# Leaky ReLU as one ScalarE activation, and the sign of float64 weights brought by the same function

## The chip, the core and the metric

The kernel runs on one core of a Trainium2 chip. The core has five engines that work side by side, each taking its own instructions strictly in order: TensorE (PE: matrix products, with PEld for its weight loads), VectorE (DVE), ScalarE (ACT), GpSimd (POOL) and SyncE (SP, which here only issues DMAs). They wait for each other by semaphores. The metric is the device time of one execution in microseconds, as the median of several runs.

## The reference

Three stages follow each other: a gated linear attention (batch 2, 8 heads, 768 steps, head size 40), a gated feed-forward part (320 to 1536 to 320) and a leaky-ReLU feed-forward part (320 to 2048 to 320), over 1536 tokens.

```python
# attention, per step t
m_new = np.maximum(f_gate[:, :, t] + m, i_gate[:, :, t])
C = f_stab[:, :, None, None] * C + i_stab[:, :, None, None] * np.einsum('bhd,bhe->bhde', vt, kt)
y[:, :, t] = o * h_tilde / denom
# first feed-forward part
g = xn @ w_gate
silu = g * (1.0 / (1.0 + np.exp(-g)))
x = silu * (xn @ w_val) @ w_out
# second feed-forward part
h = x @ w_in
g = np.maximum(0.01 * h, h)
return (g @ w_out).astype(np.float32)
```

The weights come as float64 and are turned into float32 on the core.

## The kernel before

Attention is done in 12 tiles of 128 tokens of one batch (`T` = 0 to 11), the feed-forward parts in 4 groups `g` of 384 tokens. All products are float32; in the feed-forward parts each factor is split in a high and a low part, so that one product is several matmuls.

**Attention tile.** PE makes scores `s` from `qkt`; ACT makes decay weights `w` from `Ab` (which POOL has masked), DVE multiplies `s` into `w`; PE makes `o` from `w`, `nat` and the state `Cbd`; DVE and ACT normalise it (`sm`, `y`, `junk`), POOL finishes the norm (`sm`), DVE makes `xn`, PE transposes it into `tp`, ACT and DVE copy it into `xt`. Between products of the first tiles PE gets filler products (`busy`) that nothing reads.

**First feed-forward part** (`ffn1`). For each 128 hidden columns `f` PE makes `g` and `v` (8 matmuls each), ACT a tanh `th`, DVE two products, ACT the high part `sh`, DVE the low part `sl`, and PE adds them with `wB` into `xa`. The first four `f` of each group run between the attention tiles, the other eight after them.

**Second feed-forward part** (`ffn2`). For each `f` PE makes `h` (8 matmuls), `u` is made from it, ACT makes the high part `gh`, DVE the low part `gl`, and PE adds 9 matmuls `oa`.

**Weight conversion** (`to_f32`). A float64 word arrives as two 32-bit halves in `raw` (`raw_A` 128x512, `raw_R` 128x256, `raw_B` 128x320; each has two buffers, loaded in turn by SP). DVE shifts the low half into `w32` (called `w_A`, `w_R`, `w_B` in the profile); DVE puts the sign bit of the high half to it; ACT changes the exponent of the high half in place; DVE shifts that and puts it to `w32`. Then ACT rounds it to the high part and DVE makes the low part. 58 such conversions are made: 20 of A, 10 of R, 28 of B. With `gate[0]`, the first DVE step of a conversion is kept behind an earlier DVE instruction; the ACT step is not.

**Order.** The first part is written out by hand (`HEAD`, as a manual schedule). Behind it `BODY` is a written order too, but a scheduler with its own estimate of times merges it, and all that follows, into one order for each engine, bound by data and by buffers; so any change in the instructions moves others.

Of the kernel before, what the change touches and what calls it, by code (L numbers as in the profile page):

```python
# [7 lines left out]
F32 = mybir.dt.float32  # L8
# [3 lines left out]
AF = mybir.ActivationFunctionType  # L12
# [61 lines left out]
class Engine:  # L74
    """An engine whose last instruction can be looked up, and whose next ones can be kept behind an earlier one."""

# [13 lines left out]
def body(ctx: ExitStack, tc, ig, fg, qk, nat, wgv, wgr, wo1, wi2, wi2r, wo2, rg, cst, cst2, out):  # L90
# [27 lines left out]

    # ---- constants
    ident = const.tile([128, 128], F32, name="ident")  # L120
# [12 lines left out]

    # ---- gates
    gt = [wpool.tile([16, 2, NC, L], F32, tag="wA", name=f"gt{i}") for i in range(5)]
# [12 lines left out]
    def busy(n, dst=None, start=True):  # L148
        """Keeps the tensor engine's clock up; nothing reads what it writes."""
        if n and dst is None:  # L150
            dst = psum("busy", "acc")
        for _ in range(n):
            PE.matmul(dst, idle[0], idle[1][:, 0:dst.shape[1]], start=start, stop=start)

    # F and a local to each chunk, and A over them, for chunks c0 to c1
    def scan_f(c0, c1):
# [62 lines left out]

    # ---- attention, one tile of 128 tokens of one batch at a time  # L220
    st_ = [dict() for _ in range(NTILE)]
# [29 lines left out]

    # even heads at rows 0-39 and odd heads at rows 64-103 run in different row tiles, so in different banks
    def att_qk(T, tag="s"):
# [59 lines left out]
    def att_av(T, fill=0, mid=0):  # L313
        c, b = divmod(T, B)
        t = st_[T]
        vn = t["vn"]
        o1 = psum(f"o1_{T}", "o", 2)
        spare = o1[:, H * V1:]
        t["num"] = num = o1[:, 0:H * V1].rearrange("p (h d) -> p h d", h=H)
        # one accumulation over the bank: its first product clears, the others find their columns clear  # L320
        if c > 0:
            for p in range(4):
                PE.matmul(
                    o1[:, p * 2 * V1:(p + 1) * 2 * V1], t["eb"][0:104, p, :], Cbd[b][:, p, :],
                    start=(p == 0), stop=False,
                )
            busy(mid, spare, False)
        for e in range(2):
            for p in range(4):
                PE.matmul(  # L330
                    num[:, 2 * p + e], t["w"][e][:, p, :], vn[:, 2 * p + e, :], start=(c == 0),
                    stop=(c == 0 or (e == 1 and p == 3)),
                )
                if p % 2:
                    busy(fill, spare, c == 0 or (e == 1 and p == 3))
        if c < NC - 1:
            st = o1[:, H * V1:]
            for h in range(H):
                p, e = divmod(h, 2)
                lo, hi = (0, 64) if e == 0 else (64, 104)  # L340
                PE.matmul(st[lo:hi, p * V1:(p + 1) * V1], Kt[b][:, p, lo:hi], vn[:, h, :], start=True, stop=True)
            t["stv"] = st[0:104, 0:4 * V1].rearrange("p (j d) -> p j d", j=4)
# [12 lines left out]

    # normaliser, output gate, 1 / sqrt(mean(y^2) + 1e-6)
    def att_tanh(T):
# [167 lines left out]
    def conversion(key, f):  # L525
        """The next step of one conversion; the last one leaves the weight complete."""
        if (key, f) not in convs:
            if key == "A":
                convs[key, f] = weight_a(f, raws[f][0], raws[f][1])
            else:  # L530
                convs[key, f] = weight_b(f, raws[f][2])
        return convs[key, f]
# [43 lines left out]

    # ---- weights: float64 words rounded toward zero to float32, then split in two parts that add up to it
    def load_raw(src, n, name):
# [4 lines left out]
    def to_f32(raw, n, name):  # L583
        lo, hi = raw[:, :, 0], raw[:, :, 1]
        w = conv.tile([128, 512], U32, tag="w32", name=f"w32_{name}")[:, 0:n]
        first = V.tensor_scalar(out=w, in0=lo, scalar1=29, scalar2=None, op0=ALU.logical_shift_right)
        after(first, gate[0])
        V.scalar_tensor_tensor(out=w, in0=hi, scalar=0x80000000, in1=w, op0=ALU.bitwise_and, op1=ALU.bitwise_or)
        # exponent bias 1023 -> 127, three places to the right of where float32 has it
        A.activation(hi.bitcast(F32), hi.bitcast(F32), AF.Abs, scale=2.0 ** -112)  # L590
        yield
        V.scalar_tensor_tensor(out=w, in0=hi, scalar=3, in1=w, op0=ALU.logical_shift_left, op1=ALU.bitwise_or)
        return w.bitcast(F32)
# [8 lines left out]
    def weight_a(key, raw, raw_rest):  # L602
        """256 columns of the first 256 rows; with every second, the last 64 rows of two such."""
        w = slot("wA", [128, 2, 3, 256], key % NF, f"wA_{key}")
# [20 lines left out]
    def weight_b(key, raw):  # L625
        x = yield from to_f32(raw, DM, f"B{key}")
        if key < NF:
            # high 0:256, low 256:576, high of the last 64 columns
            w = slot("wB", [128, 2 * DM], key, f"wB_{key}")
# [13 lines left out]
    def up(dst, w, m, X):  # L643
        """dst[128 m, N] = w[:, m tile].T @ x, with x and w in two parts each."""
        ms = slice(m * 128, (m + 1) * 128)
        seq = [
            (w[:, 0, 0, ms], X[:, 0]), (w[:, 0, 0, ms], X[:, 3]),
            (w[:, 0, 1, ms], X[:, 1]), (w[:, 0, 1, ms], X[:, 4]),
            (w[:, 1, 0, ms], X[:, 0]), (w[:, 1, 1, ms], X[:, 1]),
            (w[:, 0, 2, ms], X[:, 2]), (w[:, 1, 2, ms], X[:, 2]),  # L650
        ]
        for i, (a, x) in enumerate(seq):
            PE.matmul(dst, a, x, start=(i == 0), stop=(i == len(seq) - 1))

    # ---- first feed-forward part for one group
    def ffn1(g, f0, f1):
        X = xt[g]
        def terms(f, sh, sl, i):
            w = WB[f]
            if i < 2:  # L660
                wh, wl = w[:, i * 128:(i + 1) * 128], w[:, 256 + i * 128:384 + i * 128]
                return [(wh, sh), (wh, sl), (wl, sh)]
            # high and low parts of the last 64 columns side by side
            wr = w[:, 512:640]
# [58 lines left out]
        def finish():  # L723
# [4 lines left out]
            if f1 == NF:  # L728
                # the last 64 columns came in two halves
                tmp = ffn.tile([64, N], F32, tag="th", name=f"tmp{g}")  # L730
# [16 lines left out]
    def ffn2(g, f0, f1):  # L747
# [25 lines left out]
        for f in range(f0, f1):  # L773
# [3 lines left out]
            u = ffn.tile([128, N], F32, tag="th", name=f"u{g}_{f}")  # L777
            A.mul(u, ph[:, 0:N], 0.01)
            V.tensor_tensor(u, ph[:, 0:N], u, op=ALU.max)
            sh = ffn.tile([128, N], F32R, tag="sh", name=f"gh{g}_{f}", bufs=SB)  # L780
# [13 lines left out]

    # ---- the whole
    def load1(f):
# [42 lines left out]
def _layout(np, q, k, v, i_gate, f_gate, o_gate, moe_w_gate, moe_w_val, moe_w_out, moe_rms_g, moe2_w_in, moe2_w_out):  # L839
# [3 lines left out]
    def headsT(a):  # L843
        # [c, b, e (head in pair, padded to 64), d, pair, t]
        t = np.zeros((NC, B, 2, 64, 4, L), f32)
# [14 lines left out]
    def up(w):  # L860
        # [320, n, 256] -> the first 256 rows [n][128][k, m], and the last 64 of two n [n / 2][(n, row)][m]
        n = w.shape[1]
# [47 lines left out]
```

## Time and profile before

| | |
|---|---|
| runs (3), device time | 497.24, 502.96, 504.24 us; median 502.96 |
| profiled execution, first to last instruction | 502.2 us; mean granted TensorE clock 0.968 |
| PE busy | 487.8 us (97%), 3026 instructions |
| DVE busy | 345.7 us (69%), 715 instructions |
| ACT busy | 257.3 us (51%), 610 instructions |
| POOL busy | 82.3 us (16%), 130 instructions |

The profile is of one execution. Nothing but its span is known of its own time, so the sum is made against the span, which lies 0.76 us under the median of the runs. A busy PE can be a slow one: the column PEclk tells what share of the full TensorE clock was granted, 1.00 being the level of 2.4 GHz and 0.50 that of 1.2 GHz.

### The profile page before, as it was taken

How to read it: one execution, taken by the hardware profiler on the slowest of the kernel's cores; microseconds unless marked ns; L12 is line 12 of the kernel's file. 1: busy time of each engine (PE TensorE's matmuls, PEld its weight loads, DVE VectorE, ACT ScalarE, POOL GpSimd, SP SyncE). 2: the span in 40 equal slices, each digit the busy share in tenths (PEclk: the TensorE clock that was granted, in tenths of full speed). 3: DMA queues.
4: the chain of work that ended last, by engine and by line, in shares of the span. 5: the costliest groups of instructions: out<-in, count | busy, mean ns of one | idle time of the engine just before them, and what ended most of it. 6: DMA issues, size and time to landing. Idle time of an engine off the chain costs nothing.

```text
span 502.2 us, 8186 instructions
## 1 busy us (share of the span) xinstructions
PE 487.8 (97%) x3026; PEld 468.8 (93%) x3029; DVE 345.7 (69%) x715; ACT 257.3 (51%) x610; POOL 82.3 (16%) x130
## 2 busy tenths in 40 slices
PE   9998799999979999999999999999999999999996
PEld 5785689889979999999999999999999999999996
DVE  5686778799995798867758486768675834545343
ACT  1243577657663667634626272458575643433332
POOL 2375365675532000000000000000000000000000
PEclk9999896987989999999999999999999999999999
DMA  6855399576310224320302030202301000101011
GB/s 208 288 191 187 111 317 266 190 210 198 109 54 15 82 77 132 115 70 0 116 2 94 1 115 1 94 1 94 96 2 52 1 1 1 40 0 41 1 39 40
DMA packets 31113, 45.90 MB, mean 91 GB/s; under 512 B 2161, under 2 KB 20513, under 8 KB 31073
## 3 DMA queue, kind: packets, MB, share of 16 engines
q1 hardware_dynamic: 31072, 45.38, 28.4%
q8 instruction: 24, 0.39, 0.3%
q14 instruction: 17, 0.13, 0.1%
HBM read 43.31 MB, written 2.06 MB: 90 GB/s over the span
## 4 chain that ended last, share of the span: by engine, by line
PE 85%; DVE 8%; ACT 2%; issue 2%; DMA 1%; POOL 1%; DVEq 0%; POOLq 0%; SPq 0%; ACTq 0%
PE h L82 18%; PE oa L82 17%; PE g L82 13%; PE v L82 12%; PE xa L82 12%; PE o L82 7%; PE s L82 3%; PE busy L82 2%; DMA nat<-nat 1%; DVE w_B L82 1%; POOL sm L82 1%; DVE w_R L82 1%; DVE wB L82 1%; DVE xn L82 1%; PE A L82 1%
## 5 line engine op out<-in xcount | busy, mean ns | idle before, releaser
L82 PE MATMUL h<-xt,wA 128*128 128x384 f32 x512 | 102.0, 337 | 0.0
L82 PE MATMUL g<-xt,wA 128*128 128x384 f32 x384 | 85.7, 353 | 4.0 <-ACT xt L82 3.7
L82 PEld LDWEIGHTS h<-xt,wA 128*128 128x128 f32 x512 | 88.9, 188 | 0.0
L82 PE MATMUL v<-xt,wA 128*128 128x384 f32 x384 | 80.2, 343 | 0.0
L82 PE MATMUL oa<-wB,gh 128*128 128x320 f32 x384 | 77.1, 308 | 0.0
L82 PEld LDWEIGHTS g<-xt,wA 128*128 128x128 f32 x384 | 71.2, 199 | 5.6 <-ACT xt L82 4.2
L82 PEld LDWEIGHTS v<-xt,wA 128*128 128x128 f32 x384 | 70.7, 196 | 0.0
L82 PE MATMUL xa<-sh,wB 128*128 128x384 f32 x240 | 69.6, 343 | 0.8 <-DVE wB L82 0.8
L82 DVE TENSOR_TENSOR u<-h,u 128x384 f32<-128x384 f32 x64 | 35.4, 555 | 41.7 <-ACT u L82 41.5
L82 PEld LDWEIGHTS oa<-wB,gh 128*128 128x128 f32 x384 | 63.2, 188 | 0.0
L82 ACT ACTIVATE u<-h 128x384 f32<-128x384 f32 x64 | 31.5, 492 | 49.8 <-PE h L82 46.4
L82 DVE TENSOR_TENSOR gl<-u,gh 128x384 fp32r<-128x384 f32 x64 | 35.5, 556 | 26.1 <-ACT gh L82 26.0
L82 PE MATMUL oa<-wB,gl 128*128 128x320 f32 x192 | 49.3, 309 | 0.0
L82 PE MATMUL xa<-sl,wB 128*128 128x384 f32 x144 | 48.5, 337 | 0.0
L82 ACT CAST gh<-u 128x384 fp32r<-128x384 f32 x64 | 32.7, 515 | 27.4 <-DVE u L82 27.3
L82 PEld LDWEIGHTS xa<-sh,wB 128*128 128x128 f32 x240 | 44.6, 192 | 1.5 <-DVE wB L82 1.1
L82 ACT ACTIVATE th<-g 128x384 f32<-128x384 f32 x48 | 23.4, 488 | 36.2 <-PE g L82 31.9
L82 DVE SCALAR_TENSOR_TENSOR th<-th,g 128x384 f32<-128x384 f32 x48 | 26.3, 549 | 19.8 <-ACT th L82 19.4
L82 ACT CAST sh<-th 128x384 fp32r<-128x384 f32 x48 | 24.4, 512 | 28.7 <-DVE th L82 25.3
L82 DVE TENSOR_TENSOR sl<-th,sh 128x384 fp32r<-128x384 f32 x48 | 28.5, 599 | 9.6 <-ACT sh L82 9.5
L82 PEld LDWEIGHTS oa<-wB,gl 128*128 128x128 f32 x192 | 33.7, 188 | 0.0
L82 DVE SCALAR_TENSOR_TENSOR w_B<-raw_B,w_B 128x320 uint32<-128x320 uint32 x56 | 30.1, 548 | 4.7 <-ACT raw_B L82 4.5
(90 smaller groups left out, 711.2 us busy)
## 6 DMA issues: line engine op xcount, KB each, us to landing
raw_B<-wo SPq DMA_DIRECT2D x28, 320.0 KB, 3.3
qkt<-qk SPq DMA_DIRECT2D x12, 512.0 KB, 4.9
raw_A<-wgv SPq DMA_DIRECT2D x12, 512.0 KB, 3.9
nat<-nat SPq DMA_DIRECT2D x12, 484.0 KB, 5.1
Ab<-A_d SPq DMA_DIRECT2D x11, 512.0 KB, 6.5
raw_A<-wi SPq DMA_DIRECT2D x8, 512.0 KB, 3.5
eb<-e_d SPq DMA_DIRECT2D x20, 128.0 KB, 5.7
out<-x SPq DMA_DIRECT2D x12, 160.0 KB, 1.9
```

What stands on the lines that cost most here:

```text
L82: self.last = getattr(self.engine, name)(*args, **kwargs)
```

## The change

`u` in `ffn2` was made by ACT (0.01 times `h`) and DVE (the larger of that and `h`). Now one ACT instruction, a leaky activation with slope 0.01 (`Prelu`), reads `h` and writes `u`.

In `to_f32` the DVE step with the sign bit is left out. The ACT step, which took the absolute value times 2^-112, is now a leaky activation with slope -(2^32): a negative word comes out positive with 32 more in its exponent, and the last DVE step, a shift left by three places, moves that bit to the place of the sign. Loads, products and the other instructions are the same in kind and number.

```diff
@@ def to_f32
         first = V.tensor_scalar(out=w, in0=lo, scalar1=29, scalar2=None, op0=ALU.logical_shift_right)
         after(first, gate[0])
-        V.scalar_tensor_tensor(out=w, in0=hi, scalar=0x80000000, in1=w, op0=ALU.bitwise_and, op1=ALU.bitwise_or)
...
-        A.activation(hi.bitcast(F32), hi.bitcast(F32), AF.Abs, scale=2.0 ** -112)
...
+        A.activation(hi.bitcast(F32), hi.bitcast(F32), AF.Prelu, scale=2.0 ** -112, alpha=-(2.0 ** 32))
         yield
         V.scalar_tensor_tensor(out=w, in0=hi, scalar=3, in1=w, op0=ALU.logical_shift_left, op1=ALU.bitwise_or)
@@ def ffn2
             u = ffn.tile([128, N], F32, tag="th", name=f"u{g}_{f}")
-            A.mul(u, ph[:, 0:N], 0.01)
-            V.tensor_tensor(u, ph[:, 0:N], u, op=ALU.max)
+            A.activation(u, ph[:, 0:N], AF.Prelu, alpha=0.01)
```

The scheduler's order moves with it. PE's instructions are the same in kind and number, in another order; ACT has the same number of instructions, DVE 122 fewer. The first places where an engine's order differs lie in the part that is written by hand, for an ACT step that waits for its load alone can stand between the instructions of that part.

**PE where the last attention tile's `o1_11` is made** (`s11`, `tp9`, `o1` belong to attention, the rest to the first feed-forward part). Before:

```order
L82 MATMUL s11_1_1627<-qkt11_1555 128x128
L82 MATMUL tp9_1639<-ident_87,xn9_1636 128x128 x3
L82 MATMUL o1_11_1664<-Cbd1_98,eb11_1559 128x82 x4
L82 MATMUL g2_0_1680<-xt2_1158,wA_0_445 128x384 x8
L82 MATMUL xa1_0_0_1706<-sh1_2_1527,wB_2_949 128x384
L82 MATMUL v2_0_1689<-xt2_1158,wA_0_445 128x384 x8
L82 MATMUL xa1_0_0_1706<-sl1_2_1528,wB_2_949 128x384
L82 MATMUL o1_11_1664<-nat11_1562,w11_0_1599 128x41 x4
L82 MATMUL o1_11_1664<-nat11_1562,w11_1_1607 128x41 x4
L82 MATMUL xa1_0_0_1706<-sh1_2_1527,wB_2_949 128x384
```

Now:

```order
L82 MATMUL g2_0_1665<-xt2_1148,wA_0_445 128x384 x8
L82 MATMUL v2_0_1674<-xt2_1148,wA_0_445 128x384 x8
L82 MATMUL xa1_0_0_1691<-sl1_2_1515,wB_2_940 128x384
L82 MATMUL xa1_0_0_1691<-sh1_2_1514,wB_2_940 128x384
L82 MATMUL xa1_0_0_1691<-sh1_3_1578,wB_3_950 128x384
L82 MATMUL xa1_0_0_1691<-sl1_3_1579,wB_3_950 128x384
L82 MATMUL xa1_0_0_1691<-sh1_3_1578,wB_3_950 128x384
L82 MATMUL xa1_0_1_1705<-sl1_0_1423,wB_0_874 128x384
L82 MATMUL xa1_0_1_1705<-sh1_0_1422,wB_0_874 128x384
L82 MATMUL xa1_0_1_1705<-sh1_1_1488,wB_1_913 128x384
L82 MATMUL o1_11_1649<-Cbd1_98,eb11_1544 128x82 x4
L82 MATMUL o1_11_1649<-nat11_1547,w11_0_1584 128x41 x4
```

Ahead of the first of these rows stand `tp9` and one `xa1`: with it, the 16 matmuls of `g2_0` and `v2_0` and nine of `xa1`, which stood behind the start of `o1_11`, now stand between `tp9` and `o1_11`.

**ACT in the first feed-forward part, where `raw_A10` is worked on** (`raw` rows are the exponent steps, `CAST wA` and `CAST wB` the high parts of weights, `th`, `sh` those of a unit). Before:

```order
L82 CAST sh0_6_2241<-th0_6_2237 128x384
L82 ACTIVATE raw_B9_2160<-raw_B9_2160 128x320
L82 COPY x2_92<-xa3_0_2_2148 128x384
L82 ACTIVATE th0_7_2305<-g0_7_2287 128x384
L82 CAST wB_9_2177<-w32_B9_2172 128x256
L82 CAST wB_9_2177<-w32_B9_2172 128x64
L82 ACTIVATE raw_A10_2253<-raw_A10_2253 128x512
L82 CAST sh0_7_2309<-th0_7_2305 128x384
L82 CAST wA_10_2259<-w32_A10_2260 128x512
```

Now:

```order
L82 ACTIVATE th0_4_2089<-g0_4_2071 128x384
L82 CAST sh3_3_2067<-th3_3_2063 128x384
L82 CAST wA_8_2020<-rest_8_2027 64x2x256 x2
L82 CAST wA_9_2139<-rest_8_2027 64x2x256 x2
L82 ACTIVATE raw_A10_2228<-raw_A10_2228 128x512
L82 ACTIVATE raw_R12_2563<-raw_R12_2563 128x256
L82 CAST wB_8_2040<-w32_B8_2036 128x256
L82 CAST wB_8_2040<-w32_B8_2036 128x64
L82 CAST sh0_4_2093<-th0_4_2089 128x384
L82 ACTIVATE raw_B10_2232<-raw_B10_2232 128x320
L82 COPY x2_92<-xa3_0_0_2097 128x384
```

The exponent steps of `A10` and `B10` stood beside `th0_7`, next to the rest of their conversions, and `R12`'s far behind; now all three stand beside `th0_4` and wait for nothing but their loads, `raw_B10` four ACT rows behind the high part of the `wB_8` in whose raw buffer it is loaded.

**ACT in the first part** (the step of tile 1 and 2 around `tp0` and `tp1`). Before:

```order
L82 ACTIVATE sm2_460<-o1_2_413 128x8
L82 CAST wA_0_445<-w32_A0_446 128x512
L82 CAST xt0_468<-tp0_464 128x3x128
L82 CAST xt0_468<-tp1_470 128x3x128
L82 ACTIVATE raw_R0_220<-raw_R0_220 128x256
L82 ACTIVATE junk2_510,sm2_460<-y2_477 128x320
```

Now:

```order
L82 CAST wA_0_445<-w32_A0_446 128x512
L82 CAST xt0_467<-tp0_463 128x3x128
L82 ACTIVATE raw_B1_360<-raw_B1_360 128x320
L82 CAST xt0_467<-tp1_469 128x3x128
L82 ACTIVATE raw_R0_220<-raw_R0_220 128x256
L82 ACTIVATE junk2_508,sm2_459<-y2_476 128x320
```

`raw_B1`, whose step stood some 90 instructions further on, is now between the two copies into `xt0`; `raw_B0` likewise was put before `junk1`, some ten rows above these.

## Rows read from the trace of the kernel before

**Rows 1.** Windows: microseconds, busy time (instructions) by engine, granted clock, DMA share, GB/s.

```profile
78.00:89.00 11.00, 11.00 (x58) 10.37 (x58) 9.09 (x20) 9.17 (x25) 5.54 (x10) 0.54 0.91 276
89.00:102.00 13.00, 12.59 (x104) 11.95 (x104) 10.82 (x23) 8.81 (x28) 7.80 (x11) 0.99 0.55 187
102.00:105.00 3.00, 3.00 (x12) 3.00 (x12) 2.94 (x7) 1.08 (x3) 2.51 (x6) 0.50 0.78 268
105.00:118.00 13.00, 12.23 (x108) 11.15 (x108) 12.92 (x24) 9.02 (x29) 6.83 (x8) 0.99 0.79 229
118.00:126.00 8.00, 8.00 (x33) 7.71 (x33) 7.61 (x12) 5.94 (x17) 7.64 (x11) 0.57 0.37 123
...
142.50:147.00 4.50, 1.96 (x22) 1.58 (x21) 4.42 (x12) 2.40 (x8) 0.60 (x1) 0.91 0.00 0
147.00:154.00 7.00, 7.00 (x30) 7.00 (x29) 6.50 (x16) 3.06 (x9) 1.96 (x5) 0.57 0.35 124
154.00:494.00 340.00, 340.00 (x2049) 339.92 (x2049) 220.35 (x465) 171.65 (x364) 1.46 (x5) 1.00 0.14 47
```

**Rows 2.** Chain that ended last, by engine and tile, 54 to 90 and 90 to 147.

```profile
by line: PE o L82 41.4%; PE s L82 23.7%; PE g L82 19.4%; PE v L82 13.1%; PE tp L82 1.3%; DVE xt L82 1.2%; PE pg L82 0.9%; PE pt L82 0.7%; issue 0.1%
...
by line: DMA nat<-nat 12.3%; DVE w_B L82 11.9%; issue 9.2%; DVE wB L82 8.5%; DVE xn L82 7.3%; POOL sm L82 7.3%; DVE sl L82 6.4%; DVE sm L82 4.0%; DVE xt L82 3.8%; ACT w L82 3.7%; DVE w L82 3.3%; DVE wA L82 3.2%; DVE th L82 2.6%; DVE y L82 1
```

**Rows 3.** DVE groups, whole span: count, busy us, mean ns, idle before.

```profile
L82 DVE TENSOR_TENSOR u<-h,u 128x384 f32<-128x384 f32 x64 | 35.4, 555 | 41.7 <-ACT u L82 41.5
L82 DVE SCALAR_TENSOR_TENSOR w_B<-raw_B,w_B 128x320 uint32<-128x320 uint32 x56 | 30.1, 548 | 4.7 <-ACT raw_B L82 4.5
L82 DVE SCALAR_TENSOR_TENSOR w_A<-raw_A,w_A 128x512 uint32<-128x512 uint32 x40 | 29.1, 726 | 0.8 <-ACT raw_A L82 0.6
```

**Rows 4.** ACT groups, whole span, same columns.

```profile
L82 ACT ACTIVATE u<-h 128x384 f32<-128x384 f32 x64 | 31.5, 492 | 49.8 <-PE h L82 46.4 <-DVE gl L82 2.0 <-DVE w_B L82 1.3
...
L82 ACT ACTIVATE th<-g 128x384 f32<-128x384 f32 x48 | 23.4, 488 | 36.2 <-PE g L82 31.9 <-DVE sl L82 2.5 <-DVE w_A L82 1.7
...
L82 ACT ACT_TABLE_LOAD x1 | 1.3, 1283 | 0.7 <-PEq L901 0.7
```

**Rows 5.** Timeline, last unit: start, duration, engine, tile, [idle before <-releaser].

```profile
496.11 0.56 DVE L82 TENSOR_TENSOR gl<-u,gh 128x384 fp32r<-128x384 f32 x1 [0.58 <-ACT gh L82]
...
496.83 1.04 PE L82 MATMUL oa<-wB,gh 128*128 128x320 f32 x6
```

**Rows 6.** DVE groups from 90 to 147; last row: w_B, min/median/max ns, whole span.

```profile
L82 DVE SCALAR_TENSOR_TENSOR w_B<-raw_B,w_B 128x320 uint32<-128x320 uint32 x9 | 7.8, 871 | 0.0
...
L82 DVE SCALAR_TENSOR_TENSOR w_A<-raw_A,w_A 128x512 uint32<-128x512 uint32 x4 | 2.7, 674 | 0.0
...
L82 DVE SCALAR_TENSOR_TENSOR w_B<-raw_B,w_B x56: 473/485/1583, 83.8 to 400.2; 128x320 uint32<-128x320 uint32 x56
```

**Rows 7.** Timelines of DVE, ACT and PE at the end of attention.

```profile
144.76 0.69 DVE L82 SCALAR_TENSOR_TENSOR w_A<-raw_A,w_A 128x512 uint32<-128x512 uint32 x1
...
145.49 0.67 ACT L82 ACTIVATE raw_A<-raw_A 128x512 f32<-128x512 f32 x1 [1.64 <-DVE w_A L82]
...
144.88 0.52 PE L82 MATMUL tp<-ident,xn 128*128 128x128 f32 x3 [1.27 <-DVE xt L82]
146.67 1.12 PE L82 MATMUL o<-Cbd,eb 104*128 104x82 f32 x4 [1.27 <-ACT raw_B L82]
```

**Rows 8.** Timeline of ACT in the first part.

```profile
31.98 0.47 ACT L82 ACTIVATE junk<-y 128x320 f32<-128x320 f32 x1 [1.35 <-DVE y L82]
...
43.77 0.48 ACT L82 CAST xt<-tp 128x384 fp32r<-128x384 f32 x1 [0.16 <-PE tp L82]
```

**Rows 9.** ACT waits 154 to 494 (total, times, longest); DMA issue (count, KB, us to landing).

```profile
ACT u L82 <- PE h L82: 45.5, 36, 3.2
ACT th L82 <- PE g L82: 27.5, 24, 3.4
...
raw_B<-wo SPq DMA_DIRECT2D x28, 320.0 KB, 3.3
```

## The prediction

> **What bounds the kernel now.** I read first the windows, cut where the granted clock or PE's idle time changes [rows 1]. From 154 to 494 us PE is busy 340.00 of 340.00 us at the full clock. That is two thirds of the span, all of the second feed-forward part's `h` among it, and nothing but fewer matmuls can shorten it. What can be won lies before 154. There PE loses time in two ways. It stands idle: 13.00 - 12.59 = 0.41 us from 89 to 102, 0.77 us from 105 to 118, and 4.50 - 1.96 = 2.54 us from 142.5 to 147; 3.7 us in all. And it runs at the lower level (1.2 GHz): from 78 to 89 at a mean clock of 0.54, which costs 11 x 0.46 = 5.1 us of full-speed work, from 102 to 105 1.5, from 118 to 126 3.4 and from 147 to 154 3.0 us; 13.0 in all. Together 16.7 us: if all of it went, the span would be 485.5.
>
> Second the chain of waits, for the two halves of that part [rows 2]. From 54 to 90 it is PE almost alone (`o`, `s`, `g`, `v`): a faster DVE moves nothing there. From 90 to 147 it runs through DVE, 52% of the 57 us by adding the row's DVE entries, and otherwise through loads of `nat` (12.3%), POOL's `sm` (7.3%), issue (9.2%) and ACT's `w` (3.7%).
>
> So the question is what leaves DVE between 90 and 147, and whether the new order keeps PE supplied there.
>
> **The leaky ReLU.** 64 DVE instructions of 555 ns go, 35.4 us of DVE time [rows 3]. All lie in the second feed-forward part, where PE's own work hides them: ACT waits for `h` before its `u` for 46.4 us in total [rows 4], so the makers of `u` are ahead of PE and get further ahead. If that cover were gone, each would cost up to its 0.56 us. At the end of the program, where no later unit covers, the low part `gl` of the last unit ends at 496.67 and the matmuls that read the high part start at 496.83 with three rounds of PE work still ahead of them [rows 5]: PE is the bound there too. Term: 0.
>
> What a leaky activation costs on ACT no row shows. The nearest are the scaled copy it replaces, 492 ns, and a tanh on the same shape, 488 ns [rows 4]: one is arithmetic, the other a table function, and they agree, so I take the same cost. That it is faster is excluded by nothing but that agreement; that it took twice as long, 0.5 us more for each of 64 + 58 instructions, would be 61 us of ACT time, and in the long stretch ACT is busy only 171.65 of 340 us [rows 1]. There the way from `h` to `gl` would be 0.06 us shorter than now instead of 0.56. Between 90 and 147 some ten such instructions would add 5 us of ACT time, of which ACT is 3.7% of the chain. I take 0 with an upper bound of 2.
>
> **The conversions.** Half of the 56 `w_B`, 40 `w_A` and the smaller `w_R` instructions go [rows 3]. Those after 154 are hidden by PE as above: term 0. Those before 90 too, by the chain. Between 90 and 147 the rows hold nine `w_B` and four `w_A` [rows 6]; by their order the first steps among them are those of B1 to B5 and A4 and A5, and R4 comes to these. An undisturbed `w_B` takes 485 ns (the median), `w_A` 674; for R4, which is narrower than B, 0.45. So 5 x 0.485 + 2 x 0.674 + 0.45 = 4.2 us of DVE time. The nine `w_B` have a mean of 871 in this stretch and a longest one of 1583 [rows 6]. The excess falls into times in which POOL works, and I leave it on DVE: what stands next in the queue meets POOL instead. With the chain on DVE for 52% of the time, the term is 0.52 x 4.2 = **-2.2 us**. Its ends: 0, when loads and POOL take the place of every step removed, and -6.1, when all of it is on the path and the excess of five (5 x 0.386 = 1.9) goes too.
>
> The Trainium skill (SBUF — State Buffer, section "Who interferes with whom") says that a VectorE instruction with two SBUF inputs contends with a GpSimd instruction that reads SBUF, and that whichever comes second is blocked for the whole of the other. That agrees with the 485 against 1583 ns, and by it the excess stays with the next two-input instruction: 4.2 us, not 6.1, come off DVE.
>
> **The end of attention.** Here the step with the sign stands in the way itself. `w_A` of A5 at 144.76 is that step; ACT waits 1.64 us for it and starts the exponent at 145.49; behind that in ACT's queue stands `raw_B`, and PE's `o1_11` is put down to it after 1.27 us idle; before that PE waited 1.27 us for `xt` on DVE, behind the conversion's first steps [rows 7]. In the new order the exponent steps of A5 and B5 are done long before, and 25 matmuls (`g2_0`, `v2_0`, nine of `xa1`) stand between `tp9` and `o1_11`. At the pace of the long stretch, 340 / 2049 = 0.166 us each, they cover 4.1 us, more than the 2.54 us idle. So I take the whole 2.5 us. The low clock from 147 to 154 follows this idle time; I take half of its 3.0 us, since low clocks at 78, 102 and 118 came without such a gap. Term **-4.0 us**, ends 0 and -5.5. If it goes, the loads of `nat` and the `sm` chain are late next.
>
> **What moves.** An ACT exponent step now waits for its load and nothing else, and the scheduler put it early. In the first part, `raw_B0` fits into 1.35 us in which ACT is idle before `junk`; `raw_B1` stands between the two copies into `xt0`, where only 0.16 us is idle [rows 8]; at 0.49 us (as `u` in rows 4) it costs **+0.3 us** on the way to the first unit's `xt`. Bounds 0 and 0.5. From 60 to 126 steps of A2 to B5 come earlier, and loads with them (`raw_A4`, `raw_B3`, `raw_B4` and `raw_B5` now pass loads of attention on SP's queue). What that does to the stretches of low clock I can't say; bounds from one of the rows are 3.4 us either way, and I take 0.
>
> **Sum.** -2.2 - 4.0 + 0.3 = -5.9 on a span of 502.2 gives 496.3; the median of the runs lies 0.76 above the span, so **497.1 us**, 1.2% less. About 2% (10 us) is what a measurement of this kernel can tell from no change.
>
> **Rivals.** *Nothing comes of it.* After each step removed, loads of `nat`, POOL's `sm`, issue and ACT's `w` (32.5% of the chain) end as late as before, and PE's order trades one gap for another. For it: PE is 12.59 of 13 and 12.23 of 13 us busy even there [rows 1], so there is little idle time to give back. Against it: the 2.54 us gap is one that the change names. Time: 503.0 + 0.3 = 503.3.
>
> *The attention part closes up.* All 4.2 us of DVE count, and the idle times of 0.41 and 0.77 and the low clocks from 102 to 105 and 118 to 126 go, as more feed-forward work stands between attention's matmuls: -(4.2 - 2.2) - 1.2 - 1.5 - 3.4 = -8.1 against the forecast, 489.0. For it: conversions finish earlier, so units can start earlier. Against it: the attention matmuls that precede the low clocks are the same.
>
> *Slower: ACT stands waiting for loads in the long stretch.* ACT works in order, so an exponent step whose load has not landed holds up the `th`, `sh` or `u` behind it. `raw_B10` stands behind three casts, about 1.1 us after its buffer can come free, and such a load lands 3.3 us after its issue [rows 9]: 2.2 us of waiting. What PE doesn't notice is about what ACT now waits for PE before an `u` or `th`, 45.5 / 36 = 1.3 and 27.5 / 24 = 1.1 us on the mean [rows 9]. So 1.0 us over, and 43 of the 58 conversions come after 154. It decides from about 16 of them on, where 16 us outweigh the gain and the 2%; at 20 the time is 497.1 + 20 = 517. For it: nothing holds these steps back as the gate holds DVE's first. Against it: the gaps are a mean and the longest is 3.2 and 3.4, and most steps stand further behind their load than `raw_B10`.
>
> *The leaky activation is not the cheap instruction it looks like.* If it took twice as long the time would be about 499, within 2%. The Trainium skill (ScalarE: Activation LUTs, section "Table sets: the hidden batching unit") says that functions outside the active set cost a table load at each switch, and the only load in the trace takes 1283 ns [rows 4]. Two switches for each of 58 conversions would be 116 x 1.283 = 149 us of ACT time; but ScalarE's order in the changed kernel holds one table load, as before, so I give this no weight of its own.
>
> **How the numbers follow.** Forecast 0.50, nothing 0.20, closes up 0.20, slower 0.07, dearer activation 0.03. The range: the lower end is the forecast with the terms' far ends and one low clock gone, 497.1 - 3.9 - 1.5 - 3.4 = 488.3, so 488; the upper end takes in the second case with 1.2 us of the bound on the activation, 504.5. Outside are the slower case and the tails of the others. Faster by over 2% (under 492.9): the third case and 0.02 of the forecast, 0.22. Slower by over 2% (over 513): 0.06. Within 2%: 0.72.
>
> **What the profile after would show.** DVE about 71 us less busy; the new `u` at 0.49 us, and raw steps as long as before; PE still 100% at clock 1.00 from some 150 us to the end; no `o` or `tp` idle over 1 us at the end of attention, and a steady stretch that begins about 6 us earlier. Wrong would be: ACT waits on DMA for `raw` with PE idle behind them, or a new stretch of clock 0.5. The forecast is wrong upward if the gap at the end of attention only moves to another place, for the low clock moves with it.

## The result and the profile after

The changed kernel takes 506.05 us (median of 20 runs, 497.98 to 509.91), the kernel before 500.40 in the 20 runs taken beside them. The ratio of the two is **1.015** with a 95% interval of 1.010 to 1.020; by the medians it is 1.011. It is slower, by less than 2%. The forecast of 497.1 was wrong, in sign too: 5.9 us less were forecast, by the medians 5.7 us more came, and 506.05 lies above the range.

The ratio compares the runs within 1.5% of each kernel's fastest, the medians compare all of them; where the two tell different things, both are given.

The profiled execution has a span of 503.7 us and a time of 505.43. Its windows, in the order of [rows 1]: microseconds, busy time (instructions) of PE, PEld, DVE, ACT, POOL, then granted clock, DMA share, GB/s.

```profile
78.00:89.00 11.00, 11.00 (x38) 9.60 (x38) 7.72 (x18) 8.29 (x24) 4.61 (x9) 0.50 0.95 264
89.00:102.00 13.00, 9.60 (x68) 9.20 (x67) 11.41 (x23) 7.40 (x24) 7.54 (x11) 0.76 0.66 192
102.00:105.00 3.00, 3.00 (x18) 2.63 (x16) 0.56 (x1) 1.52 (x4) 0.91 (x3) 0.83 0.42 151
105.00:118.00 13.00, 12.18 (x91) 11.27 (x91) 12.25 (x20) 5.67 (x17) 8.02 (x10) 0.95 0.43 135
118.00:126.00 8.00, 8.00 (x51) 7.62 (x51) 3.44 (x8) 7.83 (x22) 1.33 (x5) 0.50 0.55 181
126.00:142.50 16.50, 15.80 (x101) 14.98 (x100) 11.20 (x19) 9.28 (x31) 11.10 (x15) 0.87 0.21 63
142.50:147.00 4.50, 4.50 (x35) 4.13 (x34) 4.05 (x10) 1.81 (x6) 2.16 (x4) 1.00 0.00 0
147.00:154.00 7.00, 6.83 (x47) 6.40 (x46) 6.48 (x11) 4.54 (x14) 2.91 (x3) 1.00 0.39 122
154.00:494.00 340.00, 340.00 (x2053) 339.94 (x2053) 171.74 (x365) 172.13 (x363) 3.14 (x10) 1.00 0.15 47
```

The gap and the low clock at the end of attention are gone, as forecast: 4.50 of 4.50 and 6.83 of 7.00 at the full clock, where [rows 1] have 1.96 and a clock of 0.57. But from 89 to 102 PE is busy 9.60 of 13.00 at a clock of 0.76, where it was 12.59 at 0.99, and from 126 to 142.5 the clock is 0.87, where it was 1.00:

```profile
126.00:142.50 16.50, 16.38 (x129) 15.73 (x127) 14.29 (x25) 11.56 (x36) 9.68 (x16) 1.00 0.27 83
```

The long stretch is what it was, 340.00 of 340.00 at 1.00. From 154 us to the end the program takes 503.7 - 154 = 349.7 us, before 348.2: PE is 1.5 us further behind when the stretch begins, not 6 us ahead.

The groups that answer to [rows 3, 4]; the first is ACT's, the next two DVE's, then ACT's exponent steps and its table load.

```profile
L82 ACT ACTIVATE u<-h 128x384 f32<-128x384 f32 x64 | 31.5, 492 | 78.3 <-PE h L82 77.2 <-PE oa L82 1.0
...
L82 DVE SCALAR_TENSOR_TENSOR w_A<-raw_A,w_A 128x512 uint32<-128x512 uint32 x20 | 15.7, 783 | 0.8 <-ACT raw_A L82 0.8
...
L82 DVE SCALAR_TENSOR_TENSOR w_B<-raw_B,w_B 128x320 uint32<-128x320 uint32 x28 | 14.4, 528 | 0.0
...
L82 ACT ACTIVATE raw_B<-raw_B 128x320 f32<-128x320 f32 x28 | 13.9, 495 | 5.0 <-DMA raw_B<-wo 4.7
...
L82 ACT ACTIVATE raw_A<-raw_A 128x512 f32<-128x512 f32 x20 | 13.5, 673 | 6.3 <-DMA raw_A<-wi 3.6 <-DMA raw_A<-wgv 2.5
...
L82 ACT ACT_TABLE_LOAD x1 | 1.3, 1283 | 0.7 <-PEq L899 0.7
```

The leaky activation costs on ACT what the scaled copy did, 492 ns, and no table load is added. ACT now waits 77.2 us for `h` where it waited 46.4: what the leaky ReLU saved became ACT's waiting. And ACT's `raw` steps wait for loads. Before, they waited for DVE's step with the sign:

```profile
L82 ACT ACTIVATE raw_B<-raw_B 128x320 f32<-128x320 f32 x28 | 13.5, 498 | 5.8 <-DVE w_B L82 5.6
L82 ACT ACTIVATE raw_A<-raw_A 128x512 f32<-128x512 f32 x20 | 13.5, 675 | 7.6 <-DVE w_A L82 7.5
```

PE's waits from 54 to 154 (total, times, longest), and DVE's timeline where the longest of them ends.

```profile
PE s L82 <- issue: 3.4, 1, 3.4
PE s L82 <- DVE w L82: 0.8, 1, 0.8
PE tp L82 <- DVE xn L82: 0.7, 1, 0.7
```

```profile
91.36 1.54 DVE L82 SCALAR_TENSOR_TENSOR xn<-y,sm,gb 128x320 f32<-128x320 f32 x1 [0.36 <-POOL sm L82]
92.82 0.54 DVE L82 SCALAR_TENSOR_TENSOR th<-th,v 128x384 f32<-128x384 f32 x1
93.28 3.28 DVE L82 TENSOR_TENSOR wB<-w_B,wB 128x256 fp32r<-128x256 f32 x4
96.49 0.68 DVE L82 TENSOR_TENSOR w<-s,w 128x512 f32<-128x512 f32 x1
```

PE stands from 93.87 to 97.27 before the scores `s8`. They go into the bank that `s7` holds until DVE's product `w` (`w7_0`) has read it, and that begins at 96.49: the profile writes "issue", but the bank comes free at about 97.2. Ahead of `w7_0` in DVE's queue stand the low parts of `wB_2` and `wB_3`, 3.28 us in this place beside POOL's work on `Ab` and `eb`. In the order of before the steps of B2 and B3 stood behind `w7_0`.

ACT's timeline near 115, where its steps wait for loads:

```profile
114.18 0.49 ACT L82 ACTIVATE th<-g 128x384 f32<-128x384 f32 x1
115.10 0.67 ACT L82 ACTIVATE raw_A<-raw_A 128x512 f32<-128x512 f32 x1 [0.42 <-DMA raw_A<-wgv]
117.97 0.44 ACT L82 ACTIVATE raw_R<-raw_R 128x256 f32<-128x256 f32 x1 [2.20 <-DMA raw_R<-wgr]
118.31 0.66 ACT L82 COPY Cbd<-C 64x164 f32<-64x164 f32 x2
```

`raw_R8`, which DVE reads at 186.75, 69 us later, stands in ACT's queue ahead of attention's `Cbd`, and ACT waits 2.20 us for its load. From 54 to 154 ACT waits 5.2 us in all for `raw` (2.2 for `raw_R`, 1.7 for `raw_A`, 1.3 for `raw_B`).

One thing must be taken out before the two spans are compared. PE's timeline in the first part, in two kernels whose order there is the same (the first experiment below, then the sixteenth):

```profile
4.48 1.03 PE L82 MATMUL busy<-const-bfloat16-1.0 128*128 128x512 bf16 x2
5.45 2.07 PE L82 MATMUL A<-gt,ident 16*128 16x128 f32 x8
7.45 1.03 PE L82 MATMUL busy<-const-bfloat16-1.0 128*128 128x512 bf16 x2
8.41 2.07 PE L82 MATMUL A<-gt,ident 16*128 16x128 f32 x8
```

```profile
4.25 0.61 PE L82 MATMUL busy<-const-bfloat16-1.0 128*128 128x512 bf16 x2
4.79 1.15 PE L82 MATMUL A<-gt,ident 16*128 16x128 f32 x8
5.87 0.61 PE L82 MATMUL busy<-const-bfloat16-1.0 128*128 128x512 bf16 x2
6.41 1.32 PE L82 MATMUL A<-gt,ident 16*128 16x128 f32 x8
```

In some executions PE runs at half speed from about 4.3 us on, in others from about 7.7, and the first unit `g0_0` (its eight matmuls, or the last seven where the first stands apart) starts some 3 us later in the kind that slows at 4.3 (53.2 to 54.1 us in five profiles) than in the kind that slows at 7.7 (48.9 to 50.9 in the other fifteen), whatever the kernel. The profile of before is of the first kind (54.09), that of after of the second (50.62). From there to the end before takes 502.2 - 54.09 = 448.1 us, after 503.7 - 50.62 = 453.1: 5.0 us more, 1.0% of the time, which is about what the medians show. The loss lies between `g0_0` and the long stretch.

What it consists of can be added up as the prediction did, in windows of 2 us from the end of `v0_0` (58.43 before, 54.77 after) to 160: the time in which PE stands idle, and its busy time times the share of the clock that was not granted. Before that gives 3.8 us of idle time and 13.4 us of low clock, after 5.4 and 16.7. The sums differ by 4.8 us, the spans from `v0_0` on by 5.2. So in these two profiles PE's waits are the smaller part of the loss, 1.5 us, and longer running at the lower level is the larger, 3.3 us. Over all twenty profiles the idle part lies between 2.2 and 6.8 us and the low clock between 6.6 and 23.8: the time from `v0_0` on goes mainly with the second (correlation 0.95, with the first 0.33).

All runs together agree. Those of the second kind can be told by their mean clock, which is 0.916 to 0.948 in their profiles and 0.958 to 0.969 in the five others; I take those under 0.955. Its median is 0.929 over 17 runs of the changed kernel and 0.937 over 94 runs of the kernel before, taken beside the experiments. The difference, 0.008 of some 503 us, is 4 us by estimate, most of the 5.7.

### The profile page after: what moved, and what is told of

The parts are those of the page before. It is cut to its first block, busy times and chain, and to the rows that moved or that the text cites. A ratio compares the mean times of both kernels' runs of the same rounds, so it can differ in the third digit from the quotient of the medians.

```text
span 503.7 us, 8025 instructions
## 1 busy us (share of the span) xinstructions
PE 488.7 (97%) x3026; PEld 469.2 (93%) x3029; DVE 286.6 (57%) x593; ACT 258.8 (51%) x610; POOL 81.4 (16%) x130
## 4 chain that ended last, share of the span: by engine, by line
PE 87%; DVE 5%; ACT 3%; POOL 2%; issue 2%; DMA 2%; DVEq 0%; POOLq 0%; ACTq 0%
PE h L82 18%; PE oa L82 17%; PE g L82 13%; PE v L82 13%; PE xa L82 12%; PE o L82 7%; PE s L82 4%; PE busy L82 2%; DVE w_R L82 1%; POOL sm L82 1%; DMA raw_R<-wgr 1%; DVE xn L82 1%; ACT w L82 1%; DMA nat<-nat 1%; PE tp L82 1%
## 5 line engine op out<-in xcount | busy, mean ns | idle before, releaser
L82 PE MATMUL h<-xt,wA 128*128 128x384 f32 x512 | 100.8, 337 | 0.0
L82 PEld LDWEIGHTS g<-xt,wA 128*128 128x128 f32 x384 | 70.0, 195 | 5.2 <-ACT xt L82 2.6
L82 ACT ACTIVATE u<-h 128x384 f32<-128x384 f32 x64 | 31.5, 492 | 78.3 <-PE h L82 77.2
L82 PE MATMUL xa<-sl,wB 128*128 128x384 f32 x144 | 49.8, 346 | 0.0
L82 PE MATMUL s<-qkt 40*128 40x128 f32 x192 | 27.9, 358 | 4.6 <-issue 3.8
L82 PE MATMUL o<-nat,w 128*128 128x41 f32 x192 | 31.9, 322 | 0.0
```

The costliest lines, as they stand in the source:

```text
L82: self.last = getattr(self.engine, name)(*args, **kwargs)
```

## The experiments

Eighteen experiments, numbered in the order in which they ran; 18 is the kernel of 8 again. Medians are this / before, run side by side.

| | kernel | medians, us | ratio, 95% |
|---|---|---|---|
| 1 | leaky ReLU alone | 501.39 / 501.62 | 0.998, 0.993 to 1.003 |
| 2 | conversions alone | 506.43 / 501.62 | 1.011, 1.007 to 1.015 |
| 3 | step waits, DVE step gone | 501.12 / 501.62 | 1.001, 0.996 to 1.005 |
| 4 | step free, DVE step kept | 510.56 / 501.62 | 1.013, 1.004 to 1.022 |
| 5 | early steps wait | 498.91 / 500.67 | 0.998, 0.994 to 1.002 |
| 6 | late steps wait | 502.69 / 500.67 | 1.003, 0.999 to 1.008 |
| 7 | late steps held in order | 503.04 / 500.67 | 1.007, 1.003 to 1.011 |
| 8 | 7, and early steps wait | 499.81 / 500.67 | 0.984, 0.976 to 0.992 (two runs) |
| 9 | `w7` first | 501.90 / 499.12 | 1.007, 1.004 to 1.011 |
| 10 | `w7` first, and 7 | 501.63 / 499.12 | 1.008, 1.004 to 1.012 |
| 11 | early A steps wait | 503.57 / 499.12 | 1.012, 1.007 to 1.017 |
| 12 | early B steps wait | 509.13 / 499.12 | none |
| 13 | loads later | 506.64 / 499.62 | 1.017, 1.012 to 1.022 |
| 14 | loads later, `w7` first | 503.88 / 499.62 | 1.008, 1.004 to 1.012 |
| 15 | steps in written order | 502.25 / 499.62 | 1.006, 1.002 to 1.011 |
| 16 | 1, with loads moved | 505.36 / 499.81 | 1.020, 1.013 to 1.027 |
| 17 | 1, with DVE steps moved | 500.07 / 499.81 | 1.012, 1.002 to 1.021 |
| 18 | 8 again | 498.58 / 499.81 | 1.004, 0.999 to 1.009 |

### Which part of the change, and what of it (1 to 4)

**1.** The kernel before with the new `u`; its conversions are as before.

> The leaky ReLU alone; the conversions are as before. Every engine's order is that of the kernel before up to the second feed-forward part. Theory (the freed exponent steps of the conversions cost the time, in the attention part): ratio to before 1.000, between 0.997 and 1.003, since 64 DVE instructions leave a stretch in which PE is the bound; PE stays at 340 of 340 us there. Rival (the dearer activation, or DVE's absence in the long stretch, costs): 1.01 or more.

**2.** The other half of the change.

> The conversion change alone; the leaky ReLU is as before. Every engine's order is that of the changed kernel up to the second feed-forward part. Theory (the freed exponent steps cost the time, in the attention part): as the changed kernel, 1.010 to 1.020, with the idle time of PE before the scores near 94 us again. Rival (the ReLU costs): 1.000.

**3.** The changed kernel, with a real wait:

```diff
-        A.activation(hi.bitcast(F32), hi.bitcast(F32), AF.Prelu, ...)
+        turn = A.activation(hi.bitcast(F32), hi.bitcast(F32), AF.Prelu, ...)
+        tc.add_manual_dep(turn.ins, first.ins.name, Sync)
```

> The changed kernel, but ACT's exponent step waits again for the first DVE step of its conversion, as it did before through the sign step; the sign step stays away. Theory (it is the freedom of the exponent step that costs, and the 58 DVE steps less are worth a little): 0.985 to 1.000. Rival (less DVE work in the conversions is what brings the conversions forward into attention's way, whatever ACT waits for): 1.010 or more. Rival (any new order lands somewhere in a band of 1.5 per cent, whichever change it comes from): no forecast beyond 0.985 to 1.015, and the losses stand at other places than in the changed kernel.

**4.** The changed kernel, with a DVE step that leaves `w` as it is:

```diff
+        V.scalar_tensor_tensor(out=w, in0=lo, scalar=0, in1=w, op0=ALU.bitwise_and, op1=ALU.bitwise_or)
         A.activation(hi.bitcast(F32), hi.bitcast(F32), AF.Prelu, ...)
```

> The changed kernel with a DVE step in each conversion that changes nothing, of the shape and inputs of the sign step but on the low half of the word, so that ACT's exponent step stays free of it: DVE has as much to do as before, ACT's step waits for its load alone. Theory (the freedom of the exponent step costs): 1.010 to 1.030, with ACT waiting for loads of raw before 160 us. Rival (less DVE work brings the conversions forward and costs): 1.000. Rival (any order lands in the band): 0.985 to 1.015, losses at other places.

The leaky ReLU is worth nothing (0.998, the long stretch 340.00 of 340), the conversions' change is the whole loss. Of the two things that it does to a conversion, the DVE work is not the one that counts: with the step gone and the wait kept the time is that of before (1.001), with the step kept and the wait gone it is that of the changed kernel or worse (1.013). The loss comes with the freedom of ACT's exponent step. What is not there: in 2, whose order is that of the changed kernel up to the second feed-forward part, PE is busy 13.00 of 13.00 from 89 to 102, and waits 2.3 us for a `w` at 113.8 instead:

```profile
89.00:102.00 13.00, 13.00 (x87) 12.42 (x85) 10.79 (x21) 8.11 (x25) 6.54 (x9) 0.80 0.54 175
113.79 1.31 PE L82 MATMUL s<-qkt 40*128 40x128 f32 x8 [2.32 <-DVE w L82]
```

One order does not lose its time at the same place in each execution. The sum is nearly the same: 4.3 us of idle time and 17.2 of low clock, 21.5 together, against 22.1 in the profile of the changed kernel.

### Which steps (5 to 8, 11, 12)

**5** and **6.** The wait of 3 for some conversions only; `BLK` is 4.

```diff
+        if int(name[1:]) < BLK:    # 6: >= BLK
+            tc.add_manual_dep(turn.ins, first.ins.name, Sync)
```

> The changed kernel, but the exponent steps of the first four hidden blocks (A0 to A3, R0, R2, B0 to B3), which belong to the written order, wait again for the first DVE step; the later ones are free. In DVE's order w7_0 stands no longer behind the low parts of wB_2 and wB_3; in ACT's order raw_A6 and raw_R8 still stand ahead of Cbd1 and w9_0, where they wait for their loads. Theory A (attention's w behind the conversions on DVE costs): 0.995 to 1.003, no long wait of s. Theory B (ACT's exponent steps waiting for loads cost): 1.008 to 1.015, with a wait of raw_R on its load of about 2 us near 118 and a clock of 0.5 behind it.

> The opposite: the exponent steps from the fifth hidden block on (A4, R4, B4 and all later) wait again for the first DVE step, the first four blocks are free. In DVE's order w7_0 still stands behind wB_2; raw_A6 and raw_R8 stand beside their own conversions again. Theory A (attention's w behind the conversions on DVE costs): 1.008 to 1.015. Theory B (ACT's exponent steps waiting for loads cost): 0.993 to 1.003 and no wait of raw_R or raw_A on a load before 150 us.

**7.** `gate[1]` is the cast `sh` (`gh`) of the unit that paces the conversion; `after` ties the order on one engine and waits for nothing.

```diff
+        after(turn, gate[1])
...
-            A.copy(sh, t1)
+            cast = A.copy(sh, t1)
...
-            gate[0] = done
+            gate[:] = done, cast
```

> As the run before this, but without a wait on DVE: each exponent step of a conversion that is paced by a unit is only kept, in ACT's order, behind the cast sh of that unit (or gh), as the gate keeps the first DVE step behind sl. SP's order of loads is that of the changed kernel, row by row. Theory B: 0.993 to 1.003, since it is the place in ACT's queue and not the missing wait that costs. Theory A, and the rival that the order of the loads costs: 1.008 to 1.015.

**8.** That, and the wait of 3 where there is no gate.

> Both: the paced exponent steps are kept behind sh in ACT's order, and those of the first four blocks wait for the first DVE step. Neither of the two places is left. Theory A or B, or both: 0.985 to 1.000, the only one of the four from which a gain over the kernel before could come. Rival (the order lands anywhere in a band, and the two places explain nothing): as likely 1.01.

**11** and **12.** The wait of 3 by name: A0 to A3, R0 and R2, or B0 to B3.

> The changed kernel, but the exponent steps of A0 to A3, R0 and R2 alone wait for the first DVE step. SP loads raw_A4 behind qkt8 again, not ahead of it, and w7_0 stands ahead of wB_2 and wB_3. Theory L (the early A steps bring loads of weights ahead of attention's): 0.995 to 1.003. Theory A: 0.995 to 1.003 too. Theory B: 1.010.

> The opposite: the exponent steps of B0 to B3 alone wait. SP still loads raw_A4 ahead of qkt8, but raw_B3 behind Ab8; w7_0 stands ahead of wB_2 and wB_3, behind the first and last steps of their conversion. Theory L with the A loads: 1.008 to 1.015. Theory A: 1.000 to 1.008, as two thirds of what stood ahead of w7_0 still does or it is shorter by the four low parts.

With the steps of the first four blocks waiting the loss is gone (5: 0.998), though the later ones are free and `raw_A6` and `raw_R8` still stand ahead of `w9_0` (though behind `Cbd1`, not ahead of it as put there). Theory B expected a wait of `raw_R` and a loss; neither came. But that these steps alone matter is not shown: with the later ones waiting and the early ones free most of the loss is gone too (6: 1.003). There theory A expected 1.008 to 1.015, as `w7_0` still stands behind `wB_2`, and theory B, which fell with 5, 0.993 to 1.003. PE waits as long before `s8` as in the changed kernel, and yet the time is nearly that of before:

```profile
99.52 1.19 PE L82 MATMUL s<-qkt 40*128 40x128 f32 x4 [3.69 <-issue]
```

With the later steps held in order 0.7% stay (7), which neither theory expected. Nor is it one group of the early steps: bound in part, A alone or B alone, the kernel is about as slow as the changed one or slower (11, 12; the six runs of 12 lie between 499.66 and 516.55, by the medians 1.020), where theories A and L expected no loss for 11, and at most 1.008 (A) and 1.015 (L) for 12. DVE's timeline in 11, and PE's where it waits:

```profile
104.95 1.77 DVE L82 SCALAR_TENSOR_TENSOR w_A<-raw_A,w_A 128x512 uint32<-128x512 uint32 x1
106.65 1.52 DVE L82 SCALAR_TENSOR_TENSOR w_R<-raw_R,w_R 128x256 uint32<-128x256 uint32 x1
...
110.81 0.68 DVE L82 TENSOR_TENSOR w<-s,w 128x512 f32<-128x512 f32 x1
```

```profile
111.59 1.61 PE L82 MATMUL s<-qkt 40*128 40x128 f32 x6 [3.30 <-issue]
```

Neither of the two places of the changed kernel is left there, but PE stands 3.3 us before the next tile's scores, and again a `w` on DVE ends the wait, behind conversions' steps stretched beside POOL: it is one kind of loss that turns up at another tile.

### The places by themselves (9, 10, 13 to 15)

**9.** A tie on DVE alone, with the conversions of B2 and B3 written behind `p.7.1` (the product `w7_1`); every order is that of the changed kernel up to there.

```diff
+            if key in (2, 3):
+                after(low1, marks["w"])    # w7_1
+                after(low2, marks["w"])
```

> The changed kernel with one tie on DVE: the low parts of wB_2 and wB_3 stand behind the two products of w7. All orders are those of the changed kernel up to that place, and SP's all the way; raw_A6 and raw_R8 still wait on ACT. Theory A (what costs is that attention's w stands behind these low parts): 0.995 to 1.005, no wait of s over 1 us from 89 to 102. Theory B (ACT waiting for loads): still 1.010 to 1.015. Theory L (what costs is that weights are loaded ahead of attention's inputs, which the freed steps of A2 and B0 to B3 bring about): still 1.010 to 1.015.

**10.** 9 and 7 together.

> The same tie, and the paced exponent steps kept behind sh in ACT's order; SP's order of loads is still that of the changed kernel. Theory A and B together: 0.990 to 1.000. Theory L: 1.005 to 1.015, as nothing has been done to the loads.

**13** and **14.** A tie on SP, alone and with that of 9.

```diff
+        if name in BEHIND:    # {"A4": 7, "R6": 7}
+            after(load, marks["Ab", BEHIND[name]])
```

> The changed kernel with one tie on SP: the loads of raw_A4 and raw_R6 stand behind that of Ab7, as in the kernel before, not ahead of it and of qkt8. Theory L (weights loaded ahead of attention's inputs cost the half that w7 did not explain): 1.003 to 1.008. If the loads do nothing: 1.010 to 1.015.

> The tie on SP and the tie on DVE (the low parts of wB_2 and wB_3 behind the products of w7) together; ACT's exponent steps are as free as in the changed kernel. Theory A with L: 0.995 to 1.003. If the loads do nothing: 1.007, as with the tie on DVE alone.

**15.** `held` is the ACT instruction written just ahead; `played` holds once the part written by hand is over.

```diff
+        held = A.last
         turn = A.activation(hi.bitcast(F32), hi.bitcast(F32), AF.Prelu, ...)
+        if A.behind is not None or played:
+            after(turn, held)
```

> The changed kernel with ACT's exponent steps tied in ACT's order alone: behind the ACT instruction written ahead of each (from the written body on; in the first part they are free). None waits for DVE. They then stand about where the kernel before has them, and the loads too. Theory (the place of the steps in ACT's queue costs, not the missing wait): 0.990 to 1.003. Rival (the wait for the first DVE step is itself what helps, by keeping DVE's conversions behind attention's work): 1.007 to 1.015.

The windows of 9 from 89 to 102 and from 118 to 126, and PE's waits from 54 to 165:

```profile
89.00:102.00 13.00, 13.00 (x90) 12.48 (x90) 9.86 (x19) 8.13 (x25) 6.21 (x8) 0.85 0.52 163
118.00:126.00 8.00, 8.00 (x43) 7.62 (x43) 5.75 (x10) 5.82 (x20) 4.82 (x8) 0.50 0.46 143
```

```profile
PE o L82 <- POOL C L82: 2.6, 1, 2.6
PE o L82 <- issue: 1.2, 1, 1.2
PE tp L82 <- DVE xn L82: 0.7, 2, 0.4
```

With `w7` first the idle time before `s8` is gone. It takes the ratio from 1.015 to 1.007, and, with the loads later, from 1.017 to 1.008: about half, twice. That this half belongs to that place is not shown. Other waits came instead, so that the idle time from `v0_0` to 160 is 4.5 us against 5.4; the low clock fell more, to 14.2 from 16.7. 7 and 15, which have no tie on DVE, lie as low (1.007, 1.006), and 6 lies lower with the wait in its profile. From 7 to 10, where ACT's late steps are in order already, the tie changes nothing (1.007, 1.008, where theories A and B together expected 0.990 to 1.000), and PE still stands 1.8 us before `s8` in the profile of 10. The order of the loads of `raw_A4` and `raw_R6` is not a cause: theory L fell with 13; the other loads were not moved. Holding the steps in their written order, with no wait, leaves 0.6% (15), between the two theories put there.

### Whether any new order costs (16 to 18)

**16** and **17.** The kernel of 1, so conversions with the sign step and no freed step, with the ties of 13 (behind `Ab8`) and of 9.

> A new order that has nothing to do with the change: the kernel of the first experiment (conversions as before, leaky ReLU on ACT), with the loads of raw_A4 and raw_R6 tied behind that of Ab8, two loads of attention later; the scheduler then merges the rest anew from about 80 us on. Theory (the freed exponent steps cost): 0.997 to 1.003, as the first experiment. Rival (the order of before is a good one among many, and any other order lands up to 1.5 per cent above it): 1.005 to 1.015.

> Another such order: the kernel of the first experiment with the low parts of wB_2 and wB_3 tied behind the products of w7 on DVE, which moves them by a few places near 100 us. Theory: 0.995 to 1.003. Rival (any other order lands above): 1.003 to 1.015.

> The kernel with the gate on ACT and the early steps waiting for DVE once more, as its runs lay between 487.6 and 507.6 us: if it is faster than before, its median is again under that of before by more than 1 us and the ratio under 0.995; if not, 0.996 to 1.004.

PE's waits in 16 from 54 to 154:

```profile
PE tp L82 <- DVE xn L82: 2.8, 1, 2.8
PE o L82 <- DVE w L82: 1.0, 1, 1.0
PE o L82 <- POOL eb L82: 0.9, 1, 0.9
```

A tie on two loads, which has nothing to do with the change, costs as much as the change did: 1.020, or 1.011 by the medians. Its waits stand at places that neither kernel had in its profile. Of 17 the medians say no change, the ratio 1.002 to 1.021; it decides nothing. 18 lies at 1.004, so 8 is not faster than before. Taken together, the kernels in which all exponent steps are free (the changed one, 2, 4, 9, 13, 14) lie at 1.007 to 1.017, those in which at least the early ones all wait for DVE (3, 5, 18) at 0.998 to 1.004, and those bound in other ways (6, 7, 10, 11, 12, 15) at 1.003 to 1.020. No version beat the kernel before; 5, the changed kernel with the early steps waiting, equals it and is 1.5% faster than the changed one by the medians' ratios (498.91 / 500.67 against 506.05 / 500.40).

## Why the prediction was wrong

**The leaky ReLU, 0: right**, by 1, and for the reason given: ACT's waits for `h` grew by 30.8 us. The price of a leaky activation: right, 492 ns for `u`, 495 and 673 for `raw_B` and `raw_A`, and one table load; the rival of a dear activation is out.

**The conversions, -2.2 us: not found.** 3 has this gain without the freed steps, and stands at 1.001 (0.996 to 1.005); 2.2 us are 0.4%, so a part of it may be there, and 6.1 us are excluded, unless the new order of 3 took them back. That the excess stays with what stands next was right in the main: the `w_A` that are left take 783 ns (726 before) and the `w_R` 910 (655), though the `w_B` 528 (548), and the four low parts that took 3.28 us beside POOL took 1.02 in the profile of 11, where POOL was idle for most of them. The Trainium skill (SBUF — State Buffer, section "Who interferes with whom") says that a VectorE instruction with two SBUF inputs contends with a GpSimd instruction that reads SBUF, and the rows agree. DVE is 59 us less busy, not 71.

**The end of attention, -4.0 us: right at its place and worth nothing.** The 2.5 us gap and the low clock behind it are gone, and both came back between 89 and 142. That is not the freed steps' doing alone: in 3 and 5, whose time is that of before, the gap is gone as well.

```profile
142.50:147.00 4.50, 4.50 (x28) 4.46 (x28) 4.45 (x13) 2.39 (x7) 0.00 (x0) 1.00 0.48 179
```

```profile
142.50:147.00 4.50, 4.50 (x33) 4.49 (x32) 4.40 (x8) 2.25 (x8) 1.09 (x1) 1.00 0.27 84
147.00:154.00 7.00, 7.00 (x47) 6.84 (x46) 4.92 (x13) 4.35 (x13) 1.28 (x4) 1.00 0.20 70
```

The prediction's last sentence named this as the way to be wrong upward, and the rival that one gap is traded for another had it at 0.20, but ended at no change.

**What moves, taken as 0: this is the step that failed.** The prediction saw that exponent steps and loads come earlier, wrote that it could not say what that does to the stretches of low clock, and put a value of 0 with bounds of 3.4 us on it. From `g0_0` on the changed kernel is 5.0 us slower. With the two terms that were to be gained, -2.2 and -4.0, the term would be +11, three times its bound. Of that, 6 to 7 us are the changed kernel's distance from 3 and 5, by the medians' ratios, and the rest are gains that don't come even where the steps wait. The distance comes with the freed exponent steps (2, 3, 4); it is gone when the early ones wait (5) and nearly gone when the late ones do (6). Against the profile of before, two thirds of the loss are time at the lower clock and one third is waits of PE. One of these is traced to a place, the 3.4 us where attention's `w7` stands behind the low parts of `wB_2` and `wB_3` on DVE; that it costs its length is not shown (6, 9). Losses of that kind (a `w` on DVE behind conversions, PE before the scores) stand in the profiles of the changed kernel, of 2, 6, 10, 11 and 13, at different tiles. No single place explains the whole: not the order of the loads that 13 moves, nor the late steps alone (7, 10), nor wholly the steps' place in ACT's queue (15).

One more explanation stands beside the freedom of the steps, and was a rival from the third experiment on: the order of before is one of the best of many, and any other order that the scheduler makes lands between it and some 2% above. For it are 16, and that none of the eighteen is faster; against it that 3, 5 and 8 are new orders too and cost nothing, while every order with all steps free costs. How much of the loss is the freedom itself, and how much that any new order tends to be worse, is left open; so is what in an order makes PE run longer at the lower clock.

**The slower rival** had the right mechanism and the wrong place. ACT does wait for `raw` in the long stretch, 7.7 us in all (4.4 for `raw_A`, 3.3 for `raw_B`), and PE loses nothing there, since ACT has 75.5 us of waiting for `h` behind it. It waits for `raw` between 54 and 154 as well, where PE is not busy throughout; holding these steps back (7) took the ratio from 1.015 to 1.007 and the waits from 5.2 to 0.9 us, but 9 reached the same with 3.3 us of such waits, so they are a part at most.

**The raw_B1 step, +0.3 us:** too small for a measurement in which the first part alone varies by 3 us; the profile after has it at 40.66 for 0.50 us between the two copies, as the order said, and `g0_0` at 50.62, against 50.51 in that of 3, where it doesn't stand there.

## What to carry to other kernels

An instruction that is removed takes its dependencies with it. In a kernel whose order a scheduler merges, ask first what each freed instruction can now overtake on its in-order engine, and price that before the work saved: here 122 DVE instructions were worth nothing measurable, and the wait that they carried 1%. When a well-tuned order is merged anew, allow for a loss of the size of the spread between such orders, which a tie that changes nothing else can show (16), and try the wait again where the saving has slack anyway (3, 5). And when a gap of PE is closed, add up idle time and low clock over the whole part before calling it a gain: here the waits were the smaller part of what changed.

## What the runs showed that was not expected

The first part has two lengths, 3 us apart, whatever the kernel: PE falls to half speed at about 4 us or at about 8 (the first kind and the second, above). In the profiles of the early fall the granted clock of the whole first part reads 1.00, though the 16 score matmuls take 2.08 us there as in the profiles that read 0.50: so at the start of a record the granted clock of a page need not be that of the matmuls; why is open. The mean clocks of 0.968 before and 0.928 after are therefore of two kinds and can't be set against each other; within one kind they can, 0.937 and 0.929.
